# A gated mix of two attention blocks: the gate's sums and the output weights' operands made in the prologue by ScalarE and GpSimd

## The chip, the cores and the metric

The kernel runs on one core of a Trainium2 chip. The metric is device time in microseconds for one launch. The kernel before took 2869.4 us (median of three runs, 2869.4 to 2871.16). The profiled execution is one more run of the same program.

## The reference

One input x of 2048 tokens and width 1024 goes through two blocks of 32 heads (32 wide each), and a gate per token mixes them. All data is f32.

```python
x = A_x
g = _sigmoid((x * gate_w).sum(-1, keepdims=True))
a = _A_ref(x, A_wqkv, A_wo)    # linear attention: phi(q) (phi(k)^T v) / (phi(q) . sum phi(k)), then @ wo
b = _B_ref(x, B_wqkv, B_wo)    # softmax attention: softmax(q k^T / sqrt(32)) v, then @ wo
return g * a + (1 - g) * b
```

phi(t) is t + 1 for t > 0 and exp(t) otherwise, plus 1e-6.

## The kernel before, in words

**Products.** Every large product is made of three matmuls (`three`, L150): each operand is split into a rounded high part, by a ScalarE copy to float32r, and a low part, by a subtraction (`split`, L294 to L296). Block B's q and k and the output product of block B use a form of Strassen's scheme with seven products (`PRODUCTS`; for the output `OPS`, L356), so their operands are sums and differences of quarter blocks.

**Prologue.** Two halves of the tokens, J = 0 and 1. For each, a *v pass* of eight steps k (`v_pass`, L401) puts the first half of B's v into all eight banks, while VectorE splits the pieces of x and makes their sums (`sides`, `split_sides`). Then come eight *quads* (`quad`, L449): each makes q or k for two groups of four heads out of seven products of 12 matmuls, in six banks in turn. While quad f runs, `beside` steps through generators, one step after each product: the weights of quad f + 1 (`quad_weights`), the last sums of x, the spills of the x pieces to HBM (`spill_rest`), and `wo_sums` (L499). That last one loads blocks of the output weights `b_wo` over GpSimd's DMA queue into the two halves of `zrep`, makes the four sums S1 to S4 with GpSimd, and stores them raw to HBM (`so_d`); a one-column copy by ScalarE and one by GpSimd (L506, L507) pace it. Weights of v and of the quads lie in a ring of half tiles (`RINGW`, 14 places). At the end of each v pass ScalarE copies the eight banks of v out (`v_out`, L359) into P1, C11, H11 and W2, four tiles that also hold the quads' sums.

**Main loop.** A planner at trace time (L1831 on) keeps a modelled time per engine (`T`) and puts together four streams in one order for every engine: `linear` (the rest of v, then block A's "kv", "q" and "o" chunks), `maxima` (scores of a head, whose row maxima VectorE reduces out of a bank, L1193), `heads_` (scores again, exp by ScalarE at L1333 into big tiles, the product with v at L1480; GpSimd adds up the exponentials at L1411 and L1415) and `output`. VectorE's work that isn't urgent is put in by `defer` with a cost. Beside these, three helpers are asked in every turn. `gate_step` (L530), in the kv chunks: it loads half rows of x and lets VectorE multiply and sum them with `gate_w` (L553), 32 times, at least 12 us apart, and ends with the sigmoid (L540 to L544). `pre_split` (L1511), in the o chunks: it loads one of 28 blocks of the seven operands of the output product, lets ScalarE copy the high part (L1530) and VectorE subtract (L1533, planned at 0.9 us like L553), and stores both to `wo_d`; all DMAs of `dma` (L168) stand on SP's one queue. `load_w_op` (L1565) loads the finished operands, two tiles of 1 MB each, into big tiles as these become free.

**Output.** For each of eight pairs of token tiles, X11 and T1 need the even blocks of o (`load_e`, into `raw_e` = mid0 and mid1), the other five products also the odd ones (`load_l`). The first NE = 3 pairs of X11 and T1 are made before the last head is done (L1723). `load_e(1)` is issued in the last unit of `linear` (L1042), and `load_e(2)` after `load_l(0)` in `output` (L1722).

Of the kernel before, what the change touches and what calls it, by code (L numbers as in the profile page):

```python
# [19 lines left out]
P = 128  # L20
DH = 32
# [18 lines left out]
GATE_STEP = 12.0  # L40
NE = 3
AHEAD_X = 3
PIECE_STEP = 13.0
# [6 lines left out]
def kernel(  # L50
# [3 lines left out]
    x: bass.AP,  # L54
# [70 lines left out]
    big = [None if i in (15, 19, 20) else big_tile(i, F32R) for i in range(NBIG)]  # L125
# [218 lines left out]
    RAW_BIG = (19, 20, 15)  # L344
    assert all(RINGW[NK + 2 * i + half] == (b, half) for i, b in enumerate(RAW_BIG) for half in range(2))
# [9 lines left out]
    so_d = {m: [dram.tile([P, C], F32, name=f"so{m}_{i}") for i in range(KH)] for m in ("S1", "S2", "S3", "S4")}  # L355
# [7 lines left out]
    def vcols(c):  # L363
        return [(2 * D + c * C, C)]

# [126 lines left out]
    def wo_piece(m, i):  # L492

        if m[0] == "S":
            return so_d[m][i]
        half, l = int(m[1]) - 1, int(m[2]) - 1
        return b_wo[(2 * i + l) * P:(2 * i + l + 1) * P, half * C:(half + 1) * C]

    def wo_sums():  # L499

        z0, z1 = halves(zrep)
        tokens = count()

        def step(*fns):
            n = next(tokens) % (C // DH)
            nc.scalar.copy(dn[0][:, n:n + 1], eps)  # L506
            nc.gpsimd.tensor_copy(dn[1][:, n:n + 1], dn[0][:, n:n + 1])  # L507
            for fn in fns:
                fn()
            for _ in range(4):  # L510
                yield

        load = lambda z, m, i: lambda: nc.gpsimd.dma_start(z, wo_piece(m, i))
        store = lambda m, z, i: lambda: nc.gpsimd.dma_start(so_d[m][i], z)
        add = lambda *a: lambda: nc.gpsimd.tensor_add(*a)
        sub = lambda *a: lambda: nc.gpsimd.tensor_sub(*a)
        for i in range(KH):
            yield from step(load(z0, "W21", i), load(z1, "W22", i))
            yield from step(add(z1, z0, z1), load(z0, "W11", i), store("S1", z1, i))
            yield from step(sub(z1, z1, z0), load(z0, "W12", i), store("S2", z1, i))  # L520
            yield from step(sub(z0, z0, z1), load(z1, "W21", i), store("S4", z0, i))
            yield from step(load(z0, "W11", i))
            yield from step(sub(z0, z0, z1), store("S3", z0, i))

    sums_w = wo_sums()

    gate_w_t = [mid[8], mid[9]]
    gate_at, gate_n = [0.0], [0]

    def gate_step():  # L530

        n = gate_n[0]
        if lin_kind[0] != "kv" or gate_at[0] is None or gate_at[0] > T["pe"] or n > 2 * NT:
            return
        if n == 0:
            for i, w in enumerate(gate_w_t):
                dma(w, bass.AP(tensor=gate_w.tensor, offset=gate_w.offset + i * C, ap=[[0, P], [1, C]]))
        gate_n[0] += 1
        if n == 2 * NT:
            nc.vector.tensor_add(g_sb, g_sb, omg_sb)  # L540
            nc.scalar.activation(g_sb, g_sb, AF.Exp, scale=-1.0)
            nc.vector.tensor_scalar_add(g_sb, g_sb, 1.0)
            nc.vector.reciprocal(g_sb, g_sb)
            nc.vector.tensor_scalar(omg_sb, g_sb, -1.0, 1.0, op0=ALU.mult, op1=ALU.add)  # L544
            use("dve", 0.4)
            return
        t, i = divmod(n, 2)
# [35 lines left out]
    for k in range(4):  # L583
        load_block(k)
# [1323 lines left out]
```

## Time and profile before

| what | value |
|---|---|
| median of the runs | 2869.4 us |
| the profiled execution, its own time | 2867.15 us |
| its span, first to last instruction | 2865.4 us |
| DMA | 471.57 MB, mean 165 GB/s |
| L553 (gate sums, VectorE) | 32 of 1970 ns on average |
| L1533 (low parts of output operands, VectorE) | 28 of 1586 ns |
| L516 and L515 (sums of output weights, GpSimd) | 12 of 1476 ns and 4 of 1284 ns |

Line numbers (L553) are those of the kernel before. "Busy" is the time an engine spends in instructions; matmuls overlap, so TensorE's time per matmul is read from counts in a window rather than from the mean of one. A window row gives the window's length, then for each engine its busy time and the number of instructions, the granted share of TensorE's clock, the busy share of the DMA engines and GB/s. A wait row reads "who waited <- for whom: total, times, longest". In a timeline row the first number is the start, the second the duration.

### The profile page before, as it was taken

Reading aid. Unit: us, or ns where it says so; the run is one execution under the profiler, and the core shown is the slowest. Engines: PE = TensorE matmul, PEld = TensorE weight load, DVE = VectorE, ACT = ScalarE, POOL = GpSimd, SP = SyncE. Lnnn points to the kernel's source line nnn. Section 1 sums busy time; section 2 is a strip of 40 time slices with the busy share of each in tenths; the row PEclk is TensorE's granted clock in tenths of the full one; section 3 lists DMA queues with packets and bytes.
Section 4 is the critical chain, followed back from the end, with each engine's and each line's share of the span. In section 5 each row is a group of like instructions: output and inputs, shape, how many; then the busy total and the mean of one; then the engine's idle time right before and its main releaser. Section 6 shows DMA issues by size and latency. Waiting matters only on the chain.

```text
span 2865.4 us, 46944 instructions
## 1 busy us (share of the span) xinstructions
PE 2814.4 (98%) x15848; PEld 2043.1 (71%) x15848; DVE 2397.1 (84%) x3838; ACT 1629.8 (57%) x3084; POOL 2007.3 (70%) x1010
## 2 busy tenths in 40 slices
PE   9999999999999999999999999999999999999999
PEld 8888888667766776666667767767766666666587
DVE  7877747889999999898988888878888998887588
ACT  5334321666666666666756666666666666556422
POOL 0211240799999999999889988889889889787000
PEclk9999999999999999999999999999999999999999
DMA  8977776444433344343434344455675667555764
GB/s 288 285 251 247 251 222 191 138 104 110 135 102 106 104 122 121 97 120 105 136 89 107 99 126 150 147 178 177 185 218 172 196 192 215 150 159 173 246 213 155
DMA packets 412379, 471.57 MB, mean 165 GB/s; under 512 B 107486, under 2 KB 235742, under 8 KB 410348
## 3 DMA queue, kind: packets, MB, share of 16 engines
q1 hardware_dynamic: 394092, 441.84, 49.9%
q0 software_dynamic: 18048, 26.75, 4.9%
q8 instruction: 126, 2.06, 0.3%
q14 instruction: 113, 0.93, 0.1%
HBM read 322.17 MB, written 131.86 MB: 158 GB/s over the span
## 4 chain that ended last, share of the span: by engine, by line
PE 89%; DVE 7%; DMA 2%; issue 1%; SPq 0%; ACT 0%; ACTq 0%; DVEq 0%
PE bank L1330 15%; PE bank L1188 15%; PE bank L154 14%; PE bank L157 14%; PE bank L159 14%; PE bank L1480 14%; DVE mx L1193 3%; DVE mid L553 1%; DVE mid L1533 1%; DVE bank L1262 1%; DVE bank L1431 1%; PE bank L1252 0%; PE bank L978 0%; SPq L171 0%; PE bank L867 0%
## 5 line engine op out<-in xcount | busy, mean ns | idle before, releaser
L1415 POOL TENSOR_TENSOR big<-big,big 128x512 f32<-128x512 f32 (+2 forms) x694 | 1659.3, 2395 | 118.1 <-ACT big L1333 75.7
L1193 DVE TENSOR_REDUCE mx<-bank 128x1 f32<-128x512 f32 x2048 | 1308.9, 683 | 260.4 <-PE bank L1188 257.8
L1333 ACT ACTIVATE big<-bank 128x512 f32<-128x512 f32 x2048 | 1180.1, 603 | 468.2 <-PE bank L1330 408.3
L1330 PE MATMUL bank<-big,big 128*128 128x512 f32 x1888 | 746.4, 397 | 17.5 <-DMA big<-ml 6.4
L1188 PE MATMUL bank<-big,big 128*128 128x512 f32 x1888 | 744.5, 394 | 18.1 <-DVE mx L1193 16.8
L154 PE MATMUL bank<-big,big 128*128 128x512 f32 x1576 | 617.9, 392 | 9.4 <-ACT big L295 7.7
L157 PE MATMUL bank<-big,big 128*128 128x512 f32 x1576 | 615.8, 391 | 0.0
L159 PE MATMUL bank<-big,big 128*128 128x512 f32 x1572 | 614.5, 391 | 0.1
L1330 PEld LDWEIGHTS bank<-big,big 128*128 128x128 f32 x1888 | 355.5, 189 | 149.8 <-issue 42.5
L1480 PE MATMUL bank<-big,mid 128*32 128x512 f32 x4096 | 456.0, 595 | 0.0
L1188 PEld LDWEIGHTS bank<-big,big 128*128 128x128 f32 x1888 | 356.3, 189 | 98.3 <-DVE mx L1193 22.5
L154 PEld LDWEIGHTS bank<-big,big 128*128 128x128 f32 x1576 | 297.3, 189 | 75.6 <-ACT big L295 8.6
L159 PEld LDWEIGHTS bank<-big,big 128*128 128x128 f32 x1572 | 296.0, 188 | 63.7 <-DMA big<-xs 0.9
L157 PEld LDWEIGHTS bank<-big,big 128*128 128x128 f32 x1576 | 297.2, 189 | 61.4 <-DVE big L296 0.2
L1480 PEld LDWEIGHTS bank<-big,mid 128*32 128x32 f32 x4096 | 143.1, 110 | 267.4 <-issue 267.1
L1431 DVE TENSOR_TENSOR bank<-bank,big 128x512 f32<-128x512 f32 x364 | 251.6, 691 | 5.0 <-ACT big L1333 2.9
L507 POOL COPY dn<-dn 128x1 f32<-128x1 f32 x24 | 16.1, 671 | 304.3 <-ACT dn L506 304.3
L295 ACT CAST big<-mid 128x512 fp32r<-128x512 f32 (+1 forms) x157 | 92.7, 617 | 124.5 <-DVE mid L1631 66.9
L1411 POOL TENSOR_TENSOR big<-big,big 128x1536 f32<-128x1536 f32 (+1 forms) x31 | 123.9, 3997 | 46.9 <-ACT big L1333 46.8
L296 DVE TENSOR_TENSOR big<-mid,big 128x512 fp32r<-128x512 f32 (+1 forms) x157 | 106.2, 691 | 57.9 <-ACT big L295 57.6
L154 PE MATMUL bank<-big,xh 128*128 128x512 f32 x376 | 148.0, 394 | 0.8 <-DMA xh<-xs 0.8
L157 PE MATMUL bank<-big,xh 128*128 128x512 f32 x376 | 147.6, 393 | 0.0
(150 smaller groups left out, 2226.3 us busy)
## 6 DMA issues: line engine op xcount, KB each, us to landing
big<-xs SPq DMA_DIRECT2D x288, 256.0 KB
big<-qk SPq DMA_DIRECT2D x690, 64.0 KB
xh<-xs SPq DMA_DIRECT2D x144, 256.0 KB
qk<-mid SPq DMA_DIRECT2D x128, 256.0 KB
big<-oA SPq DMA_DIRECT2D x84, 256.0 KB
xs<-big SPq DMA_DIRECT2D x64, 256.0 KB
oA<-mid SPq DMA_DIRECT2D x64, 256.0 KB
big<-big POOLq DMA_DIRECT2D x50, 256.0 KB, 5.4
```

Of the source, the lines that this page charges most:

```text
L154: yield nc.tensor.matmul(ps, sh, mh_, start=(kt == 0), stop=False)
L157: yield nc.tensor.matmul(ps, sh, ml_, start=False, stop=(late and last))
L159: yield nc.tensor.matmul(ps, sl, mh_, start=False, stop=last)
L296: eng.tensor_sub(lo, src, f32(hi))
L1188: nc.tensor.matmul(bank[b], q[:, t % TPC * P:(t % TPC + 1) * P], k[:, j * C:(j + 1) * C], start=True, stop=True)
L1193: nc.vector.tensor_reduce(m[:, t, j:j + 1], bank[b], AX.X, ALU.max)
L1330: nc.tensor.matmul(bank[b], k[:, t * P:(t + 1) * P], q_cols(h, j), start=True, stop=True)
L1333: nc.scalar.activation(pr_t[i][:, j * C:(j + 1) * C], bank[b], AF.Exp, scale=SCALE)
L1411: nc.gpsimd.tensor_add(lacc[:, :qp], pr(0)[:, :qp], pr(1)[:, :qp])
L1415: nc.gpsimd.tensor_add(lacc[:, sl], lacc[:, sl], pr(t)[:, sl])
L1431: nc.vector.tensor_add(lacc[:, qp:] if t == NT - 1 else l_b[:, :n], l_b[:, :n], src)
L1480: nc.tensor.matmul(av_b[j * DH:(j + 1) * DH, :], v[:, t, :], pr(t)[:, j * C:(j + 1) * C], start=(t == 0), stop=(t == NT - 1))
```

## The change

The gate. `gate_step` and the input x in token order go. The host hands over `gate_w` as 128 x 8, and it is loaded once. In both v passes ScalarE multiplies each raw piece of x^T (features on the partitions) by its column of `gate_w`, and GpSimd adds these up in the halves of `zrep` (`gate_add`): 16 copies and 14 additions in each half J. In quad 0, after its third product, eight matmuls of f32 with one column of ones sum over the partitions into bank 6 (`gate`). So that the products may be read before `sides` overwrites the pieces, `sides` and `split_sides` of the first v pass come one step later.

The output weights. `wo_sums` and `pre_split` become `wo_parts`: in the quads of each half J, for two of the four i, ScalarE copies each of the seven operands' high part, GpSimd subtracts, and GpSimd's queue stores both to `wo_d`. There is one pair of places for high and low, the second half of big15, which leaves the ring with 13 places. One piece is made every three steps (`PIECE_STEP`). The spills of x take seven steps for every four parts.

The output. `load_e(1)` goes to a second pair of tiles and is issued beside `load_e(0)`, `load_e(2)` where `load_e(1)` was, ahead of `load_l(0)`. S2 and S4 are loaded when `load_l(0)` has been issued, and S4, S2 stand ahead of S3 in the list.

```diff
-GATE_STEP = 12.0
-PIECE_STEP = 13.0
+PIECE_STEP = 3
...
-    RINGW = [(14, 0), (14, 1), (16, 0), (16, 1), (17, 0), (17, 1), (18, 0), (18, 1), (19, 0), (19, 1),
-             (20, 0), (20, 1), (15, 0), (15, 1)]
+    RINGW = [(16, 0), (16, 1), (17, 0), (17, 1), (19, 0), (19, 1), (14, 0), (14, 1), (20, 0), (20, 1), (15, 0),
+             (18, 0), (18, 1)]
...
+    gate_wt, gate_sum, gate_b = kvb[:, 0, :NK], halves(zrep), bank[6]
+    def gate(J):
+        yield
+        yield
+        for t in range(2 * TPC):
+            nc.tensor.matmul(gate_b[:, t:t + 1], gate_sum[t // TPC][:, t % TPC * P:(t % TPC + 1) * P], ones[:, :1],
+                             start=True, stop=True)
+        g = g_sb[:, 2 * TPC * J:2 * TPC * (J + 1)]
+        nc.scalar.activation(g, gate_b[:, :2 * TPC], AF.Exp, scale=-1.0)
+        yield
...
+    gate_t = [C11, H11, P1, W2]
+    def gate_add(raws, k):
+        for jj in range(2):
+            acc, raw, w = gate_sum[jj], raws[jj + 2 * (k % 2)], gate_wt[:, k:k + 1]
+            to = gate_t[(2 * k + jj) % len(gate_t)] if k else acc
+            nc.scalar.activation(to, raw, AF.Copy, scale=w)
+            if k:
+                nc.gpsimd.tensor_add(acc, acc, to)
...
-    def wo_sums():
+    def wo_parts(i0, i1):
         z0, z1 = halves(zrep)
+        hi_w, lo_w = (big[15][:, i * C:(i + 1) * C] for i in (2, 3))
+        def load(z, m, i, **add):
+            if i < i1:
+                nc.gpsimd.dma_start(z, wo_piece(m, i), **add)
+        def part(m, i, z):
+            nc.scalar.copy(hi_w, z)
+            nc.gpsimd.tensor_sub(lo_w, z, f32(hi_w))
+        def out(m, i):
+            for p, src in enumerate((hi_w, lo_w)):
+                nc.gpsimd.dma_start(wo_d[m][p][:, i * C:(i + 1) * C], f32(src))
+            for _ in range(PIECE_STEP):
                 yield
...
+        for i in range(i0, i1):
+            part("W11", i, z1)
+            nc.gpsimd.tensor_sub(z1, z1, z0)
+            load(z0, "W22", i, accum_op=ALU.add)
+            yield from out("W11", i)
+            part("S3", i, z1)
+            load(z1, "W11", i)
+            yield from out("S3", i)
+            part("S1", i, z0)
+            nc.gpsimd.tensor_sub(z0, z0, z1)
+            load(z1, "W12", i)
+            yield from out("S1", i)
+            part("S2", i, z0)
+            yield from out("S2", i)
+            part("W12", i, z1)
+            nc.gpsimd.tensor_sub(z1, z1, z0)
+            load(z0, "W22", i)
+            yield from out("W12", i)
+            part("S4", i, z1)
+            load(z1, "W11", i + 1)
+            yield from out("S4", i)
+            part("W22", i, z0)
+            load(z0, "W21", i + 1)
+            yield from out("W22", i)
...
     def spill_rest(J):
+        part = 0
         for name in ("X11", "X21", "X22"):
-            yield from spill(J, name)
+            for _ in spill(J, name):
+                part += 1
+                for _ in range(2 if part % 4 else 1):
+                    yield
...
+        gate_add(raw_x0[k // 2], k)
         v_pass(0, k, V_BANKS[0], range(TPC) if k == 0 else None)
-        if k % 2:
-            sides(raw_x0[k // 2], k // 2)
-        elif k:
-            split_sides(raw_x0[k // 2 - 1], 0, k // 2 - 1)
+        if k >= 2:
+            i = k // 2 - 1
+            if k % 2:
+                split_sides(raw_x0[i], 0, i)
+            else:
+                sides(raw_x0[i], i)
...
-    quads(0, lambda: load_pair(raw_x1[0], 1, 0), spill_rest(0), sums_w)
+    quads(0, lambda: load_pair(raw_x1[0], 1, 0), spill_rest(0), gate(0), wo_parts(0, KH // 2))
...
                 if k == 0 and n + 3 == len(units):
                     load_e(0)
+                    load_e(1)
...
-                    load_e(1)
+                    load_e(2)
...
-              "S2": lambda: over["lin"], "S4": lambda: over["lin"],
+              "S2": lambda: raw_l[0], "S4": lambda: raw_l[0],
...
-    w_next = ["W11", "S1", "W12", "S3", "S4", "S2", "W22"]
+    w_next = ["W11", "S1", "W12", "S4", "S2", "S3", "W22"]
```

More of the change, by code (lines that the diff above doesn't have):

```diff
@@ L342, in halves @@
         return [t[:, i * C:(i + 1) * C] for i in range(t.shape[1] // C)]
-    RAW_BIG = (19, 20, 15)
-    assert all(RINGW[NK + 2 * i + half] == (b, half) for i, b in enumerate(RAW_BIG) for half in range(2))
+    RAW_BIG = (20, 15, 18)
+    assert not {b for b, _ in RINGW[:NK]} & set(RAW_BIG)
     raw_big = [halves(big_tile(b, F32)) for b in RAW_BIG]
@@ new lines, in wo_parts @@
+        yield
+        yield
+        yield
+        load(z1, "W11", i0)
+        load(z0, "W21", i0)
+        for _ in range(PIECE_STEP):
+            yield
+        for i in range(i0, i1):
[22 more added lines that the diff above has]
+            yield from out("W22", i)
@@ L726, in split_v1 @@
         split(wpart(k, 0), wpart(k, 1), raw, nc.vector)
-    quads(1, lambda: load_v1(raw_a, range(KH)), spill_rest(1), sums_w)
-    for _ in sums_w:
-        pass
+    quads(1, lambda: load_v1(raw_a, range(KH)), spill_rest(1), gate(1), wo_parts(KH // 2, KH))
     load_v1(raw_b, range(KH, NK))
```

115 lines of the change are left out of this document (23 added, 92 removed).

## The prediction, on record before the change was run

> **What bounds the kernel now.** I read the page first, for who ends last.
>
> ```profile
> span 2865.4 us, 46944 instructions
> PE 2814.4 (98%) x15848; PEld 2043.1 (71%) x15848; DVE 2397.1 (84%) x3838; ACT 1629.8 (57%) x3084; POOL 2007.3 (70%) x1010
> PE 89%; DVE 7%; DMA 2%; issue 1%; SPq 0%; ACT 0%; ACTq 0%; DVEq 0%
> ```
>
> TensorE sets the end: it is idle for 51 us (2865.4 less 2814.4), and the chain leaves it for VectorE for 7% of the span. So the change can win no more than those idle stretches, and what the clock loses after them. The view of cores gives the second, and a table of windows says where both lie.
>
> ```profile
> core 0: 2865.4 us, clock 0.994
> ```
>
> ```profile
> core 0: us, PE busy (x) PEld busy (x) DVE busy (x) ACT busy (x) POOL busy (x), PEclk, DMA share, GB/s
> 0.00:50.00 50.00, 48.93 (x211) 40.94 (x212) 40.15 (x66) 27.43 (x49) 0.71 (x6) 1.00 0.91 300
> 50.00:200.00 150.00, 150.00 (x664) 124.20 (x663) 112.33 (x168) 57.69 (x114) 30.97 (x43) 1.00 0.82 262
> 200.00:246.00 46.00, 46.00 (x204) 38.10 (x203) 35.77 (x57) 21.71 (x38) 0.00 (x0) 1.00 0.77 248
> 246.00:400.00 154.00, 154.00 (x681) 127.52 (x680) 116.27 (x176) 58.82 (x115) 44.06 (x56) 1.00 0.75 242
> ...
> 500.00:1500.00 1000.00, 978.96 (x6210) 683.74 (x6211) 898.45 (x1487) 647.50 (x1255) 907.57 (x447) 0.99 0.41 114
> 1500.00:2080.00 580.00, 579.77 (x3396) 415.21 (x3395) 494.27 (x819) 380.47 (x730) 525.58 (x229) 1.00 0.49 146
> 2080.00:2600.00 520.00, 503.34 (x2801) 343.06 (x2800) 452.80 (x693) 326.46 (x584) 446.97 (x196) 0.99 0.64 187
> ...
> 2700.00:2760.00 60.00, 52.29 (x217) 42.05 (x216) 37.96 (x59) 14.56 (x26) 0.00 (x0) 0.94 0.84 274
> ```
>
> Clock 0.994 over the span is 17 us lost. The prologue (to 400 us) has no idle TensorE at all; one matmul costs 154/681 = 0.226 us there, so a step of the v pass (24) 5.4 us and a product of a quad (12) 2.7 us. Idle time stands in three places: 21.0 us in 500 to 1500, where the gate's sums run; 16.7 us in 2080 to 2600, where the pieces of the output weights are split; 7.7 us at 2700 to 2760, the start of the output. Between them, 1500 to 2080, with neither, it is 0.2 us in 580. That clean stretch is the strongest argument for a gain. Next, what ended TensorE's waits, and which VectorE instructions are long:
>
> ```profile
> PE bank L1188 <- DVE mx L1193: 16.8, 7, 3.1
> PE bank L154 <- ACT big L295: 7.7, 2, 6.5
> PE bank L1330 <- DMA big<-ml: 6.4, 2, 5.2
> PE bank L1330 <- DVE mx L1193: 4.4, 4, 2.5
> PE bank L1330 <- DVE mid L1265: 3.9, 4, 1.4
> ```
>
> ```profile
> L553 DVE SCALAR_TENSOR_TENSOR mid<-mid,mid x32: 681/1589/4790, 519.0 to 1442.5; 128x512 f32<-128x512 f32 x32
> ```
>
> ```profile
> L1533 DVE TENSOR_TENSOR mid<-mid,mid 128x512 fp32r<-128x512 f32 x28 | 44.4, 1586 | 0.0
> L542 DVE TENSOR_SCALAR g_sb<-g_sb 128x16 f32<-128x16 f32 x1 | 3.3, 3260 | 0.3 <-ACT g_sb L541 0.3
> ```
>
> ```profile
> 1171.19 4.67 DVE L553 SCALAR_TENSOR_TENSOR mid<-mid,mid 128x512 f32<-128x512 f32 x1
> ```
>
> ```profile
> 1171.04 4.26 POOL L1411 TENSOR_TENSOR big<-big,big 128x1536 f32<-128x1536 f32 x1
> ```
>
> The two last fences are VectorE and GpSimd at the same moment: the gate's sum, 0.68 us at best, sits until GpSimd's long add has ended (1171.04 + 4.26 = 1175.3). The row maximum queued behind it (L1193) then frees its bank late. The hand-written order gave each of these 0.9 us.
>
> **The change, part by part.**
>
> *Gate out of the kv stage.*
>
> ```profile
> 500.00:519.00 19.00, 16.53 (x69) 12.64 (x69) 12.12 (x21) 11.49 (x23) 4.32 (x3) 1.00 0.87 284
> ```
>
> 32 L553 and L542 go, with 32 loads of x. Idle 21.0 us less the 2.5 us (19.00 - 16.53) that lie before the first L553 at 519: 18.5. Clock: 0.99 over 1000 us can be 5 to 15 us; I take 6. **Gain 24** (18 to 28). The Trainium skill ("TensorE: Matmul & The Clock Gate", HAM oscillation) lets the clock fall only after idle gaps over about 3.4 us; by it these waits, 3.1 us at most, would cost no clock and the term would be 18. The row's 0.99 speaks against it.
>
> *Pieces out of the o stage.*
>
> ```profile
> 2424.85 1.26 SPq L171 DMA_DIRECT2D woS<-mid  x2
> ...
> 2428.65 1.46 SPq L171 DMA_DIRECT2D big<-mh  x2
> ```
>
> 28 copies, 28 L1533, 28 loads and 56 stores on SP's queue go. Of 16.7 us idle, 6.4 wait for the DMAs of ml, which follow those of mh at 2428.65 on SP; before them stand the pieces' stores with 1.26 us among others, and I count 2 us of the wait as theirs. The other 10.3 are waits for VectorE, 9 of them put down to L1533. With 4 us of clock (0.99 over 520): **gain 15** (9 to 20).
>
> *Blocks of o earlier.* At 2714 ScalarE waits for a block that SP issued late:
>
> ```profile
> 2698.66 8.71 SPq L171 DMA_DIRECT2D xh<-oB  x3
> 2707.42 3.75 SPq L171 DMA_DIRECT2D mid<-oB  x4
> ```
>
> ```profile
> 2714.57 0.62 ACT L295 CAST big<-mid 128x512 fp32r<-128x512 f32 x1 [12.68 <-DMA mid<-oB]
> ```
>
> load_e(2) is the last of those; it stood behind load_l(0), whose xh places were not yet free. Now it goes ahead of both load_l(0) and S2, S4. The stretch lost 7.7 us idle and 0.06 x 60 = 3.6 of clock. What is late next: the 8 MB of S4, S2, S3 and W22 (two tiles of 128x2048 f32 each), which must now land 11 us sooner at 274 GB/s (84% DMA). **Gain 8** (3 to 11).
>
> *Gate matmuls.* 16 of f32 with one moving column, each two records as L961's are.
>
> ```profile
> L1480 PE MATMUL bank<-big,mid 128*32 128x512 f32 x4096 | 456.0, 595 | 0.0
> L978 PE MATMUL bank<-ident,mid 128*128 128x128 f32 x128 | 19.4, 274 | 0.0
> L961 PE MATMUL bank<-mid,ones 128*128 128x256 f32 x8 | 2.4, 378 | 0.0
> ```
>
> Per record 0.11, 0.15 and 0.30 us; 32 records make 3.6 to 9.6; L978 is nearest in its weights. They run in the prologue, where TensorE has no gap. **Loss 5.**
>
> *Gate sums in the two v passes.* Per pass 16 ScalarE copies and 14 GpSimd adds of 128x512, the size of these:
>
> ```profile
> L515 POOL TENSOR_TENSOR zrep<-zrep 128x512 f32<-128x512 f32 x4 | 5.1, 1284 | 0.0
> ```
>
> ```profile
> 152.71 0.68 DVE L434 TENSOR_TENSOR xh<-mid,xh 128x512 f32<-128x512 f32 x1
> 153.31 0.69 DVE L296 TENSOR_TENSOR big<-extra,big 128x512 fp32r<-128x512 f32 x1
> 153.91 1.78 DVE L437 TENSOR_TENSOR mid<-xh,mid 128x512 f32<-128x512 f32 x1
> ```
>
> ```profile
> 153.40 1.75 POOL L516 TENSOR_TENSOR zrep<-zrep 128x512 f32<-128x512 f32 x1
> ```
>
> An add of GpSimd amid VectorE's subtractions costs VectorE 1.1 us (1.78 against 0.69). In the first pass VectorE has no room:
>
> ```profile
> 10.00:47.50 37.50, 37.50 (x167) 31.03 (x167) 36.84 (x59) 21.64 (x40) 0.00 (x0) 1.00 0.96 319
> ```
>
> ```profile
> 46.55 2.03 ACT L360 COPY mid<-bank 128x512 f32<-128x512 f32 x4
> ...
> 240.77 2.63 ACT L360 COPY mid<-bank 128x512 f32<-128x512 f32 x4 [0.75 <-PE bank L159]
> ```
>
> ScalarE frees the banks of v (L360) only after the last casts of quad 0's weights, which follow VectorE; and the copies write P1, C11, H11, W2, where the gate's products now lie until GpSimd has added them. So at least 13 adds must be done: 13 x 1.1 = 14.3 us late. The first copy ended at 47.1, and TensorE, with 208 of its 211 records done, wanted the bank at 50 - 3 x 0.226 = 49.3: slack 2.2, **loss 12** (0 if GpSimd fits between, 14 at most). In the second pass the records 1073 and on (of 211 + 664 + 204 at 246 us) want bank 2 at 244.5, the third copy, ended by 242.7: slack 1.8. VectorE works 35.77 of 46 us there, so part of the adds fits; but the adds and the wait for the stores of P1 and W2 (some 2 us) delay the loads of quad 0's weights too. **Loss 10** (0 to 15). Both waits are long enough to drop the clock as at 2700 (3.6 us there); **loss 4** for both. The Trainium skill ("SBUF — State Buffer", Who interferes with whom) says that a VectorE instruction with two SBUF inputs and a GpSimd one that reads SBUF hold the shared port whole, one after the other; it speaks against this change: at a whole 1.28 us per add both passes together would lose 5 us more. The 1.78 us row bears out most of it.
>
> *Pieces in the quads.* Per block i seven pieces, each a ScalarE copy (0.62), a GpSimd subtraction (1.3, 1.75 when contended), two stores, one pair of places. The next copy must wait for the landing of the last store of hi. The old stores and loads beside zrep took:
>
> ```profile
> DMA to landing us min/median/max: 2.3/4.8/6.4
> ```
>
> Copy to landing: three pieces with a second subtraction and a load 4.4 + L, three with a load 2.8 + L, one 2.2 + L, so 23.8 + 7L per block, against 21 products of TensorE, 56.7 us. L 4.8 gives 57.4: just even. With 40 more stores of 256 KB (10 MB over 300 us, 35 GB/s on 242 to 262) L may be 5 to 5.5: 2 to 6 us late per block, four blocks, and each half hides about 6 us, since a product's bank is wanted again three products after it is released. The 24 extra subtractions fall on VectorE, busy 75% there, and are hidden. **Loss 3** (0 to 20).
>
> **Sum:** 24 + 15 + 8 = 47 won, 5 + 12 + 10 + 4 + 3 = 34 lost: 13 us less. The profiled execution took 2867.15 us (span 2865.4), so 2854 for one like it; the median shown is 2.25 us above it, so **2856 us**.
>
> **Rivals.** *Slower, by the pair hi and lo.* If stores land in 6.4 us, the maximum above, a block takes 68.6 us, 11.9 more than TensorE's; four blocks less 12 us hidden lose 36 instead of 3: 2889. It decides from L = 5.7 on, where the pieces lose 16 and the 13 us are eaten. For it: DMA share is 0.82 where the pieces go, and the stores triple. Against it: the median of 4.8, and spills now spread over more of the quads. *All hidden.* If GpSimd's adds slip between VectorE's instructions and the pass absorbs them, only the gate's 5 us remain lost: 2869.4 - 47 + 5 = 2827. For it: TensorE has no gap in 400 us, so the order has some reserve. Against it: 36.84 of 37.5 us. *Cancelled.* If other VectorE work takes the place of L553 and L1533 in front of the maxima, half of 39 us stays: 2876; with the losses a little smaller, no change, 2869. Against it: the clean 580 us, in which VectorE is 85% busy too. *It doesn't do as it says* in one point: S3 and W22 still load late, so that the output wins 3 instead of 8; 2861, inside the forecast.
>
> **Chances.** The forecast with its bounds (2840 to 2862) 0.42; all hidden 0.2; cancelled 0.17 (0.15 of it within 0.2%); slower by the pair or by both passes at their upper ends 0.21. Faster means below 2863.7: 0.62; within 0.2% (5.7 us, about what a measurement of this kernel tells from no change) 0.15; slower 0.23. The range takes in the hidden case and most of the slow one: 2828 to 2885.
>
> **What would show it.** Windows of the changed kernel: TensorE idle in 500 to 1500 below 5 us, in 2080 to 2600 below 8; no wait over 2 us on ACT L295 in the output. Against that, a wait of TensorE for ScalarE's copies out of v near 50 and near 245, about 10 us each, and a prologue some 34 us longer. If the prologue ends within 8 us of before, the port term is wrong; if the kv stage still idles 15 us, it was not L553; if ScalarE waits on the stores of hi for over 3 us each, the pair decides.

## The result, and the profile after

The changed kernel takes **2875.45 us** (median of 12 runs, 2868.85 to 2881.64), the kernel before 2869.4 in the same session (12 runs, 2865.07 to 2872.05): ratio 1.0021, 95% interval 1.0011 to 1.003. It is slower by 6 us where 13 us less were forecast. The profiled execution took 2881.64 us, the slowest of its twelve, so what follows adds up to +14.5 us and not to +6.

The page of the changed kernel, the same three lines that the prediction began with:

```profile
span 2879.9 us, 46927 instructions
PE 2815.7 (98%) x15880; PEld 2051.5 (71%) x15880; DVE 2348.8 (82%) x3745; ACT 1649.3 (57%) x3093; POOL 2073.2 (72%) x1078
PE 80%; DMA 3%; DVE 1%; issue 1%; SPq 1%; ACT 0%; POOL 0%; ACTq 0%; DVEq 0%; POOLq 0%
```

TensorE still sets the end, and still has 64 us without work. They have moved, as the table of windows shows (busy time and instructions of PE, PEld, DVE, ACT, POOL, then granted clock, DMA share, GB/s):

```profile
0.00:50.00 50.00, 46.12 (x188) 36.44 (x189) 41.10 (x46) 30.94 (x54) 23.55 (x20) 0.97 0.71 234
...
420.00:500.00 80.00, 76.63 (x323) 62.07 (x322) 37.76 (x54) 21.17 (x38) 37.62 (x55) 0.96 0.82 242
500.00:1500.00 1000.00, 996.87 (x6273) 709.81 (x6272) 859.42 (x1442) 628.35 (x1217) 860.15 (x430) 1.00 0.41 113
...
2080.00:2600.00 520.00, 516.70 (x2966) 355.26 (x2959) 434.71 (x696) 326.84 (x579) 454.90 (x202) 1.00 0.55 152
2700.00:2760.00 60.00, 52.03 (x239) 38.74 (x238) 31.96 (x50) 17.63 (x33) 0.00 (x0) 0.91 0.83 280
```

In the two stages that the change was to clear, TensorE is now almost full at clock 1.00: from 500 to 1500 it idles 3.1 us in place of 21.0, from 2080 to 2600 3.3 in place of 16.7. The start of the output is as bad as it was. What is new stands in the prologue. TensorE's waits in the changed kernel (us in total, times, longest) and the four matmuls that waited longest:

```profile
PE bank L152 <- ACT mid L357: 17.4, 2, 8.9
PE bank L152 <- ACT big L293: 12.8, 2, 8.0
PE bank L152 <- DVE mid L506: 11.1, 2, 6.0
PE bank L152 <- DMA xh<-xs: 5.4, 2, 3.1
```

```profile
63.28 0.80 PE L152 MATMUL bank<-big,big 128*128 128x512 f32 x1 [8.49 <-ACT mid L357]
...
171.16 0.76 PE L152 MATMUL bank<-big,big 128*128 128x512 f32 x1 [6.01 <-DVE mid L506]
...
291.86 0.79 PE L152 MATMUL bank<-big,big 128*128 128x512 f32 x1 [8.90 <-ACT mid L357]
...
2736.03 0.79 PE L152 MATMUL bank<-big,big 128*128 128x512 f32 x1 [7.97 <-ACT big L293]
```

L357 is the copy that frees a bank of v at the end of each v pass (L360 before), L506 is the sum by which VectorE empties the bank of a quad's third product, a bank that quad 5 of a half waits for, and L293 is the cast of a split. No wait for the row maxima is left.

A ledger finds the same matmul, by its count (without the gate's own), in both traces and compares its start time. A stage has the same matmuls in both, some in another order:

| stretch | lost (+) or won (-), us | forecast |
|---|---|---|
| first v pass | +13.8 (its end at 49.5, now 63.3) | +12 |
| quad 0 of both halves: gate matmuls, and slow matmuls behind the passes | +6.6 | +5, and 4 of clock |
| quads 1 to 7, both halves | +11.0 and +8.9 | +3 |
| second v pass | +18.5 | +10 |
| first linear chunk (v), after the quads | +6.5 | 0 |
| kv stage | -28.6 | -24 |
| q stage | +2.6 | 0 |
| o stage | -25.4 | -15 |
| output | +0.6 | -8 |
| sum | +14.5 | -13 |

In quad 0 the gate's matmuls themselves take 1.84 us in each half, 3.7 in all (the first half's here); the other 2.9 us are matmuls behind the long wait at the end of a pass, at a granted clock of 0.50 until 66.1 and until 294.8:

```profile
72.93 1.84 PE L370 MATMUL bank<-ones,zrep 128*128 128x1 f32 x16
```

The two stages won more than the idle time in their windows. Cut at the same matmuls, the kernel before (first fence) and the changed one (second) show why; the rows are the kv and the o stage:

```profile
504.00:1705.40 1201.40, 1181.25 (x7487) 827.70 (x7486) 1076.71 (x1790) 785.81 (x1522) 1100.75 (x546) 1.00 0.41 113
...
2121.70:2695.60 573.90, 557.94 (x3146) 374.11 (x3145) 488.77 (x747) 358.12 (x647) 450.40 (x190) 0.99 0.61 183
```

```profile
569.30:1742.10 1172.80, 1170.86 (x7487) 827.10 (x7486) 1016.76 (x1722) 784.46 (x1521) 1089.58 (x546) 1.00 0.40 108
...
2161.00:2709.50 548.50, 547.33 (x3146) 371.53 (x3145) 451.12 (x719) 347.43 (x619) 441.70 (x190) 1.00 0.53 152
```

The same 3146 matmuls of the o stage have 14.8 us less of idle time (16.0 to 1.2), and are themselves 10.6 us shorter (557.94 to 547.33). In the kv stage it is 18.2 and 10.4. Part of this is the clock: a wait can be followed by slow matmuls (the section on why the prediction failed shows one). The rest isn't told apart here.

### The profile page after: what moved, and what is told of

It is laid out like the page before. It is cut to its first block, busy times and chain, and to the rows that moved or that the text cites. A ratio compares the mean times of both kernels' runs of the same rounds, so it can differ in the third digit from the quotient of the medians.

```text
span 2879.9 us, 46927 instructions
## 1 busy us (share of the span) xinstructions
PE 2815.7 (98%) x15880; PEld 2051.5 (71%) x15880; DVE 2348.8 (82%) x3745; ACT 1649.3 (57%) x3093; POOL 2073.2 (72%) x1078
## 4 chain that ended last, share of the span: by engine, by line
PE 80%; DMA 3%; DVE 1%; issue 1%; SPq 1%; ACT 0%; POOL 0%; ACTq 0%; DVEq 0%; POOLq 0%
PE bank L1358 16%; PE bank L1216 16%; PE bank L1508 15%; PE bank L152 10%; PE bank L155 10%; PE bank L157 10%; DMA woS<-big 1%; DMA v<-mid 1%; PE bank L1280 1%; SPq L169 1%; PE bank L1006 0%; PE bank L895 0%; DMA xh<-mid 0%; DMA xh<-xs 0%; DVE big L294 0%
## 5 line engine op out<-in xcount | busy, mean ns | idle before, releaser
L1443 POOL TENSOR_TENSOR big<-big,big 128x512 f32<-128x512 f32 (+2 forms) x694 | 1641.7, 2370 | 108.2 <-ACT big L1361 65.3
L152 PEld LDWEIGHTS bank<-big,big 128*128 128x128 f32 x1576 | 299.1, 190 | 112.5 <-ACT mid L357 18.2
L294 DVE TENSOR_TENSOR big<-mid,big 128x512 fp32r<-128x512 f32 (+1 forms) x157 | 119.5, 777 | 61.2 <-ACT big L293 61.1
L533 POOL TENSOR_TENSOR big<-zrep,big 128x512 fp32r<-128x512 f32 x28 | 37.2, 1330 | 171.6 <-ACT big L532 94.1
L293 ACT CAST big<-mid 128x512 fp32r<-128x512 f32 (+1 forms) x157 | 92.5, 616 | 108.0 <-DVE mid L1627 66.7
```

Of the source, the lines that this page charges most:

```text
L152: yield nc.tensor.matmul(ps, sh, mh_, start=(kt == 0), stop=False)
L294: eng.tensor_sub(lo, src, f32(hi))
L1443: nc.gpsimd.tensor_add(lacc[:, sl], lacc[:, sl], pr(t)[:, sl])
```

## Experiments

The first theory, from that ledger: **(a)** GpSimd's additions for the gate hold VectorE up and make both v passes late; **(b)** ScalarE, waiting for the stores of the one pair hi and lo to land, makes quad 5 late; **(c)** the output's start is bound by something that loading blocks of o earlier doesn't touch. The rivals: any added work in the passes does it, GpSimd's subtractions in the quads do it, or the new order of loads does it. Ratios are to the kernel before in the same session; "us" is the median.

### What makes the v passes late

**e1**, no additions:

```diff
             nc.scalar.activation(to, raw, AF.Copy, scale=w)
-            if k:
-                nc.gpsimd.tensor_add(acc, acc, to)
```

> The changed kernel without the 28 GpSimd additions of the gate's sums (the gate's sums are then those of the first block alone); ScalarE's 32 copies, their places P1 and W2, and the gate's matmuls stay. Theory: the additions, amid VectorE's dense subtractions of the two v passes, hold VectorE up (1.7 to 1.8 us instead of 0.69 each), and that is 11 of the 13.8 us lost in the first pass and about 10 of the 18.5 in the second: 2854 us (2849 to 2860), TensorE's 8.65 us stall at 63 gone. Rival: ScalarE's copies and their wait for the stores of P1 and W2 carry the loss of the passes: within 5 us of the changed kernel, 2870 to 2876, and the stall at 63 stays.

Measured: 2844.47 us, ratio 0.9928 (0.9909 to 0.9946). The first pass ends at 48.8, 0.7 us *earlier* than in the kernel before, with all of ScalarE's 16 new copies in it; the second pass loses 5.8 in place of 18.5. The theory's sign holds, and its size was short: by the ratios (1.0021 to 0.9928) e1 wins 27 us on the changed kernel, not 21. The same group of VectorE's subtractions in the first pass, in the changed kernel and in e1 (busy us, mean ns, then idle time):

```profile
L294 DVE TENSOR_TENSOR big<-big,big 128x512 fp32r<-128x512 f32 x22 | 21.8, 1040 | 3.7 <-ACT big L293 3.7
```

```profile
L294 DVE TENSOR_TENSOR big<-big,big 128x512 fp32r<-128x512 f32 x22 | 13.9, 687 | 3.6 <-ACT big L293 3.6
```

The count and the shapes are the same; the mean is 1040 ns with the additions and 687 without.

**e9**, additions without copies:

```diff
-            to = gate_t[(2 * k + jj) % len(gate_t)] if k else acc
-            nc.scalar.activation(to, raw, AF.Copy, scale=w)
             if k:
-                nc.gpsimd.tensor_add(acc, acc, to)
+                nc.gpsimd.tensor_add(acc, acc, raw)
```

> The changed kernel with GpSimd's 28 additions of the gate reading the raw blocks of x directly, and without the 28 copies of ScalarE that weight them (the gate's sums then lack their weights). No addition waits for a copy and no copy for a place. Theory: it is the additions beside VectorE's subtractions that cost the time: the first pass again loses 12 to 14 us (TensorE's stall at 63 stays), and the second wins back the 8 us of the wait for P1 and W2: 2867 us (2863 to 2872). Rival: it is the chain copy, addition, free place, next copy on ScalarE's queue that is late: as without any additions, 2844 to 2852 us.

Measured: 2866.76 us, ratio 0.9995 (0.9985 to 1.0004), on the theory's number. Without the 28 copies the first pass loses 13.4, as much as with them; the second loses 11.4. So the chain of copies and places is not the cause in the first pass. The windows of the first pass in the changed kernel, in e9 and in e1, each from 10 us to its end:

```profile
10.00:63.00 53.00, 42.09 (x173) 32.76 (x171) 50.78 (x59) 30.27 (x54) 22.84 (x14) 0.93 0.68 227
```

```profile
10.00:62.90 52.90, 42.74 (x172) 33.66 (x170) 51.02 (x59) 22.63 (x41) 23.17 (x14) 0.93 0.69 231
```

```profile
10.00:48.80 38.80, 38.80 (x173) 32.02 (x172) 36.90 (x59) 29.79 (x55) 0.00 (x0) 1.00 0.93 311
```

Read the third and the fifth pair of figures: the same 59 VectorE instructions take 36.90 us beside no GpSimd work and 50.78 or 51.02 beside 14 additions, 1.0 us more for each addition. The Trainium skill ("SBUF — State Buffer", Who interferes with whom) calls the port that the two engines share an exclusive lock; these rows agree in kind, at 1.0 us for an addition whose shortest took 1.3 us (L390).

In the second pass 18.5 less 11.4 is what the copies add: they write P1 and W2, whose last products are still being stored. The changed kernel's ScalarE and VectorE there:

```profile
242.76 0.72 ACT L388 ACTIVATE mid<-xh,kvb 128x512 f32<-128x512 f32 x1 [7.21 <-DMA qk<-mid]
```

```profile
244.82 0.69 DVE L405 TENSOR_TENSOR xh<-xh,mid 128x512 f32<-128x512 f32 x1 [8.36 <-ACT mid L388]
```

ScalarE's copy waits 7.2 us for a store, and VectorE 8.4 us for the copy. The prediction gave this wait "some 2 us". ScalarE's waits for these stores are shorter where the pieces are out of the quads (2.1 us in e6, below, against 7.8 in all here), and there the pass loses 12.7. So the pieces, too, lengthen the second pass; how they delay those stores isn't shown.

**e3**, the sums by VectorE alone:

```diff
-            to = gate_t[(2 * k + jj) % len(gate_t)] if k else acc
-            nc.scalar.activation(to, raw, AF.Copy, scale=w)
             if k:
-                nc.gpsimd.tensor_add(acc, acc, to)
+                nc.vector.scalar_tensor_tensor(acc, raw, w, acc, op0=ALU.mult, op1=ALU.add)
+            else:
+                nc.scalar.activation(acc, raw, AF.Copy, scale=w)
```

> The changed kernel with each of the 28 later gate pieces done by one VectorE multiply-add (scalar_tensor_tensor) into the sum in place of ScalarE's copy and GpSimd's addition; everything else as changed. Theory of the additions' hold on VectorE: an instruction of VectorE's own takes 0.7 us where an addition of GpSimd costs 1.1, and the wait for the places P1 and W2 goes, so the passes get back 4 and 12 us: 2860 us (2855 to 2867). Rival: what counts in the passes is any work on VectorE's side at 98% busy, so that 0.7 us more per piece costs as much as before: 2870 to 2876 with the gain of the places at most 5.

Measured: 2858.26 us, ratio 0.9965 (0.9954 to 0.9977): as the theory had it, and already faster than the kernel before. The passes lose 7.6 and 8.8. In e9, which hasn't the copies either, they lose 13.4 and 11.4. So 28 more instructions of 0.75 us on VectorE, full as it is, cost less than 28 additions on GpSimd beside it.

### What each half of the change is worth

**e4**, the gate back in the kv stage (the core of the diff):

```diff
     def gate_add(raws, k):
 
+        return
         for jj in range(2):
...
+        gate_step()
         fold_now()
```

> The changed kernel with the gate as it was before: 32 VectorE sums over loads of x in the kv stage; no gate piece and no gate matmul in the prologue. Theory: the gate's part of the change costs the prologue 38 to 40 us (13.8 + 18.5 in the passes, 6.5 in the matmuls) and wins 28.6 in the kv stage, so that undoing it wins about 10: 2865 us (2859 to 2870), the kv stage again with some 21 us of idle TensorE between 500 and 1500. Rival: the kv stage's gain is the change's whole gain and the passes are late for the new order of loads and sides, not for the gate: slower than the changed kernel, 2880 to 2900.

Measured: 2871.02 us, ratio 1.0014 (1.0005 to 1.0024), 1 us above the expected interval. By the ledger the prologue and the first linear chunk lose 26.2 without the gate and 65.3 with it, and the kv stage wins nothing without it: 39.1 paid for 28.9 in these profiles. By the ratios e4 wins only 2 us on the changed kernel, and the two intervals overlap.

**e6**, the pieces back in the o stage:

```diff
-    def wo_parts(i0, i1):
+    def wo_sums(i0, i1):
...
+        pre_split()
         load_w_op()
```

> The changed kernel with the pieces of the output weights as they were before (GpSimd sums S1 to S4 beside the quads, hi and lo made in the o stage by ScalarE and VectorE, with their loads and stores on SyncE's queue); the gate stays in the prologue as changed. Theory: the pieces cost the prologue about 23 us (quads 5 and 7 of the first half 10, quad 5 of the second 8, the first products after it 6) and won 25 in the o stage: undoing them gives 2874 to 2881 us, the stalls of TensorE at 171 and 399 gone, and some 16 us of idle in the o stage back. Rival (the prediction's step): pieces in the quads cost 3: 2890 to 2897.

Measured: 2870.15 us, ratio 1.0006 (0.9996 to 1.0015). Neither number: the pieces cost 30.0 by the ledger (65.3 less 35.3), more than the 23 expected, and won 24 in the o stage, where e6 loses all but 1.2 of the 25.4. The rival (3 us) is out by far. So **each half of the change gives back about what it wins**: the pieces alone (e4) leave the kernel 4 us slower than before, and the gate alone (e6) can't be told from no change.

### What makes quad 5 late

The chain behind TensorE's wait of 6.01 us at 171.16 in the changed kernel, on ScalarE and then on VectorE:

```profile
166.15 0.62 ACT L532 CAST big<-zrep 128x512 fp32r<-128x512 f32 x1 [3.88 <-DMA woW<-big]
...
167.31 1.64 DVE L294 TENSOR_TENSOR big<-mid,big 128x512 fp32r<-128x512 f32 x1 [2.36 <-ACT big L293]
...
170.32 0.69 DVE L506 TENSOR_TENSOR mid<-bank,mid 128x512 f32<-128x512 f32 x1
```

ScalarE's copy of a piece waits for a store to land, the next cast stands behind it, VectorE waits for that cast, and the sum that frees the bank comes late.

**e2**, stores that don't hold the pair:

```diff
-            for p, src in enumerate((hi_w, lo_w)):
-                nc.gpsimd.dma_start(wo_d[m][p][:, i * C:(i + 1) * C], f32(src))
+            for p in range(2):
+                nc.gpsimd.dma_start(wo_d[m][p][:, i * C:(i + 1) * C], wo_piece("W11", i))
```

> The changed kernel with its 56 stores of pieces reading a block of b_wo in DRAM in place of the pair hi and lo (as many stores of as many bytes; the output's operands are then wrong), so that ScalarE's next copy does not wait for the landing of the last. Theory: the wait of ScalarE for the landing of the stores (55 us over 28 pieces) makes ScalarE and then VectorE late in quads 5 of both halves and costs about 18 us: 2858 us (2853 to 2864), the stalls of TensorE at 171 and 399 gone. Rival: the 52 GpSimd subtractions that the pieces do hold VectorE up, and the wait is hidden: no change, 2870 to 2876.

Measured: 2850.29 us, ratio 0.9939 (0.9924 to 0.9954). Quads 1 to 7 lose 0.0 us in both halves in place of 11.0 and 8.9, with all of GpSimd's subtractions still there. The rival falls. The ledger also has the second v pass at 13.8 in place of 18.5 and the first linear chunk at 0.1 in place of 6.5, neither of which the expectation counted.

**e8**, a second pair, at the price of one place of the ring:

```diff
-    RINGW = [(16, 0), (16, 1), (17, 0), (17, 1), (19, 0), (19, 1), (14, 0), (14, 1), (20, 0), (20, 1), (15, 0),
-             (18, 0), (18, 1)]
+    RINGW = [(16, 0), (16, 1), (17, 0), (17, 1), (19, 0), (19, 1), (14, 0), (14, 1), (20, 0), (20, 1), (18, 0),
+             (18, 1)]
...
+            hi_w, lo_w = pairs[0]
+            pairs.reverse()
```

> The changed kernel with two pairs of places for hi and lo, taken in turn (the second pair is a place of the weights' ring, which then has 12 in place of 13). Theory: ScalarE's wait for the landing of the stores of hi (3.6 to 8.0 us a store) is what the pieces cost: with a second pair a piece's copy waits for the stores of the piece before the last, 9 us earlier, the stalls of quads 5 go, and the time is 2855 us (2850 to 2861). Rival one: GpSimd's 52 subtractions hold VectorE up: 2872 to 2877. Rival two: the ring with 12 places makes the weights of a quad late and eats the gain: over 2864, with new waits of TensorE for VectorE in the quads.

Measured: 2917.68 us, ratio 1.0168 (1.0153 to 1.0183): rival two, far beyond what it named. TensorE's waits in e8:

```profile
PE bank L152 <- ACT big L293: 43.2, 17, 8.8
...
PE bank L157 <- DVE big L294: 11.7, 11, 2.5
```

Of the seventeen waits for casts fifteen stand at the second product of a quad, one in nearly every quad. With 12 places the weights of the next quad come late, as the rival had it. On the pair itself this run says nothing.

**e10**, the same places and the same work, the stores issued earlier:

```diff
             nc.scalar.copy(hi_w, z)
+            nc.gpsimd.dma_start(wo_d[m][0][:, i * C:(i + 1) * C], f32(hi_w))
             nc.gpsimd.tensor_sub(lo_w, z, f32(hi_w))
+            nc.gpsimd.dma_start(wo_d[m][1][:, i * C:(i + 1) * C], f32(lo_w))
...
-            for p, src in enumerate((hi_w, lo_w)):
-                nc.gpsimd.dma_start(wo_d[m][p][:, i * C:(i + 1) * C], f32(src))
```

> The changed kernel with the stores of a piece issued earlier on GpSimd's queue: that of hi right behind ScalarE's copy, that of lo right behind its subtraction, both ahead of the piece's second subtraction and load. Same work, same places, same ring of 13. Theory of the landing wait: ScalarE gets the place of hi back 2 to 4 us earlier per piece, which is most of its 55 us of waits; the stalls of quads 5 shrink or go: 2859 us (2851 to 2866). Rival: the subtractions of GpSimd hold VectorE up and the wait is hidden: 2872 to 2877.

Measured: 2853.69 us, ratio 0.9961 (0.9946 to 0.9976). The answer for ScalarE's copy of a piece, L532, in the changed kernel (its waits, us and times) and in e10:

```profile
L532 ACT CAST big<-zrep x28: 612/621/623, 90.3 to 439.3; 128x512 fp32r<-128x512 f32 x28
...
its engine sat idle before it (us, times) until:
  DMA woS<-big: 30.6, 12
  DMA woW<-big: 24.7, 10
```

```profile
L532 ACT CAST big<-zrep x28: 613/616/622, 90.0 to 415.7; 128x512 fp32r<-128x512 f32 x28
...
its engine sat idle before it (us, times) until:
  DMA woS<-big: 0.6, 1
```

55.3 us of waits in 22 copies became 0.6, and quads 1 to 7 lose 0.0 us in both halves. Theory (b) is shown from both sides: e2 takes the wait away, e10 shortens what stands before it.

### Where the output's 8 us went

**e5**, the kernel before with the output part alone:

```diff
                     load_e(0)
+                    load_e(1)
...
-    raw_e = (mid[0], mid[1])
+    raw_e = [(mid[0], mid[1]), (mid[3], mid[4])]
...
-    w_next = ["W11", "S1", "W12", "S3", "S4", "S2", "W22"]
+    w_next = ["W11", "S1", "W12", "S4", "S2", "S3", "W22"]
```

> The kernel before with only the change's output part: the second and third blocks of o load earlier (into mid 3 and 4 and before load_l(0)), S2 and S4 may load earlier and the output weights load in the order W11, S1, W12, S4, S2, S3, W22. Theory: the start of the output is bound by the landing of the bytes of the weights and blocks (DMA share 0.84 before, 0.83 after the change in 2700 to 2760), so the order alone moves nothing: 2867 to 2872 us, with 6 to 9 us of idle TensorE there again. Rival (the prediction's step): the block that ScalarE waited 12.7 us for comes in time and the stretch wins 8: 2859 to 2863.

Measured: 2869.99 us, ratio 1.0003 (0.9994 to 1.0012): nothing, as theory (c) had it. The block that ScalarE waited 12.7 us for is in time, and the next one isn't. SyncE's queue and ScalarE in e5:

```profile
2704.37 2.54 SPq L171 DMA_DIRECT2D big<-woS  x4
...
2708.65 6.58 SPq L171 DMA_DIRECT2D xh<-mid  x1
```

```profile
2720.82 0.62 ACT L295 CAST big<-xh 128x512 fp32r<-128x512 f32 x1 [6.44 <-DMA xh<-mid]
```

The issue of the last head's rows of the block (xh<-mid, a transfer of 16 KB from tile to tile, `load_rest`) takes 6.6 us on the queue, behind 4 MB of weights. Two runs on top of the version with both cures (n1, below) tell whether it is the queue or the bytes. **e11** and **e12**:

```diff
-            dma(to[LAST, KH - 1], avs[j * DH:(j + 1) * DH, i * P:(i + 1) * P])
+            nc.gpsimd.dma_start(to[LAST, KH - 1], avs[j * DH:(j + 1) * DH, i * P:(i + 1) * P])
```

> The version with both cures (2838 us, 0.9906 of the kernel before) with one edit: the small transfers of the last head's rows into the blocks of o (load_rest) are issued on GpSimd's queue, which is idle there, in place of SyncE's, where one of them waits 5.2 us behind the weights S2 and S3 before it is issued. Queue theory: ScalarE's wait of 6.9 us for it shrinks by most of those 5 us: 2833 us (2830 to 2835), ratio to before 0.988 to 0.9895. Rival, the DMA engines are full (share 1.04 at 2680 to 2690): the rows land no earlier, within 2 us of 2838, ratio 0.990 to 0.9915.

```diff
-              "S2": lambda: raw_l[0], "S4": lambda: raw_l[0],
-              "S3": lambda: st_done[0] == steps,
+              "S2": lambda: raw_l[0] and not rest_left, "S4": lambda: raw_l[0],
+              "S3": lambda: st_done[0] == steps and raw_l[0] and not rest_left,
-              "W22": lambda: over["head"] and pr_idle(slot(H - 1, NT - 6), slot(H - 1, NT - 5))}
+              "W22": lambda: over["head"] and raw_l[0] and not rest_left and pr_idle(slot(H - 1, NT - 6), slot(H - 1, NT - 5))}
```

> The same version with another edit: the weights S2, S3 and W22 (2 MB each) load only when the last head's rows have been sent for, on the same queue. Theory of the bytes ahead: the rows land some 5 us earlier and ScalarE's wait shrinks, but the weights are late in their turn; on balance 2834 us (2831 to 2837). Rival: the first product with S2 or S3 waits as long as the wait that goes: 2837 to 2845.

Measured: e11 **2831.58 us**, ratio 0.9879 (0.9862 to 0.9895), against 0.9906 for n1, the queue theory's number; e12 2840.15, 0.9906 (0.9891 to 0.9921), no gain. In e11 GpSimd issues the same transfer at once, and ScalarE's cast doesn't wait at all:

```profile
2678.06 0.55 POOL L1611 DMA_DIRECT2D xh<-mid  x1 [64.82 <-ACT mid L1671]
```

```profile
2685.72 0.62 ACT L293 CAST big<-xh 128x512 fp32r<-128x512 f32 x1
```

with the DMA engines as full as ever:

```profile
2680.00:2690.00 10.00, 8.81 (x38) 6.63 (x38) 4.47 (x8) 2.96 (x6) 0.10 (x1) 1.00 1.04 382
```

By the ledger the output is 8.6 us shorter in e11 than in the kernel before, and as long as there in e12; all four runs of e11 lie below all four of e12 in the same session. So theory (c), as e5's expectation put it (bound by bytes), is wrong: it was a small transfer's place in a queue. In e12 the rows are in time too, but the rows of block A's output (`ra`) now stand behind the weights. SyncE's queue, VectorE and ScalarE there:

```profile
2677.09 2.39 SPq L169 DMA_DIRECT2D big<-woS  x4
...
2681.66 0.85 SPq L169 DMA_DIRECT2D big<-ra  x2
```

```profile
2698.34 0.75 DVE L1680 SCALAR_TENSOR_TENSOR big<-mid,omg_sb,big 128x512 f32<-128x512 f32 x1 [9.00 <-DMA big<-ra]
```

```profile
2701.18 0.62 ACT L293 CAST big<-xh 128x512 fp32r<-128x512 f32 x1 [12.05 <-DVE xh L1627]
```

VectorE's wait for `ra` is 2.1 us in e11. On one queue the order here only chose who waited.

### Versions that follow

**n1** is e3 and e10 together.

> Both cures in one: the gate's sums by one VectorE multiply-add per piece, and the stores of hi and lo issued right behind the instructions that make them. Theory: the two losses lie in different stretches (passes and quads 5) and their cures add, 17 and some 16: 2842 us (2834 to 2850), faster than both kernels. Rival: VectorE's multiply-adds make the passes late by what the earlier stores win, so that no more than the larger of the two is seen: 2855 to 2860.

Measured: **2838.03 us**, ratio 0.9906 (0.9891 to 0.992): the cures add, since they lie in different stretches. Its first product of the first linear chunk starts at +23.6 against the kernel before (+58.8 in the changed kernel), and the kv and o stages keep their 28.7 and 25.7. With e11's edit, 1.2% below the kernel before, it is the fastest version here.

**n2** and **b2** put the gate's sums into the first linear chunk, n2 on e10's stores, b2 on the kernel before (the lines of b2; n2 has the same `gate_step`):

```diff
-        if lin_kind[0] != "kv" or gate_at[0] is None or gate_at[0] > T["pe"] or n > 2 * NT:
+        if lin_kind[0] not in ("v", "kv") or lin_done[0] < GATE_FROM or gate_at[0] > T["pe"] or gate_free[gate_n[0] % 2] is None or gate_free[gate_n[0] % 2] > T["pe"] or n > 2 * NT:
...
-        xn, to = mid[10], (g_sb, omg_sb)[i]
+        xn, to = gate_x[n % 2], (g_sb, omg_sb)[i]
```

In both, the two places of gate_x also hold v of the first two heads, which the loads of x overwrite, so that part of the attention is computed from other values; the amount of work is the same.

> The changed kernel with the stores of a piece issued earlier, and with the gate taken out of the prologue and put into the first linear chunk (v, between the quads and the kv stage), as VectorE sums over loads of x as in the kernel before, one each 2.6 us with two places in turn. Theory: VectorE is busy 50% there and GpSimd does no long additions, so the 32 sums cost nothing but the contention of their 8 MB of loads with those of x (DMA share 0.73 there): the gate's 33 us in the prologue go, the kv stage keeps its gain, 2830 us (2822 to 2842). Rival: the added loads make the x of the linear chunk late (a wait of 3.3 us for it is there already), 10 to 25 us: 2842 to 2860.

> The kernel before with one edit: the 32 sums of the gate run in the first linear chunk (v) in place of the kv stage, one each 2.6 us with two places in turn. Nothing else of the change. Theory: the kv stage's 18.5 us of idle TensorE and its clock go (the changed kernel won 28 there) and the chunk hides the sums: 2844 us (2838 to 2856). Rival: the loads of x collide with those of the chunk and half or more is given back: 2856 to 2868.

Measured: n2 2846.84 us, 0.9935 (0.9918 to 0.9951); b2 2858.99, 0.9973 (0.9963 to 0.9982). Both are faster than the kernel before, both by the rival's account. TensorE's first waits in n2:

```profile
PE bank L156 <- DMA xh<-xs: 10.0, 2, 8.8
...
PE bank L156 <- DMA big<-xs: 5.8, 2, 3.3
```

The chunk's own x comes late behind the gate's loads: n2 loses 19 us between its first product and the kv stage, b2 18. Compared with n1 (0.9906), the prologue, where x is in SBUF anyway, is the better place.

## Why the prediction failed, step by step

- **"Pieces in the quads, loss 3 (0 to 20)"** is the step that failed most: 20 us in the quads, and 30 for the pieces in all (e6), with what they add to the second v pass (5.8) and with some 6 in the first linear chunk, whose cause is open (below). Its formula came near and its L was too small. From a median of 4.8 for the old stores and loads it took 5 to 5.5, and said that from 5.7 on the pair decides. The stores of hi and lo in the changed kernel:

```profile
L537 POOL DMA_DIRECT2D woS<-big x32: 539/539/565, 104.6 to 433.5; - x32
...
DMA to landing us min/median/max: 2.8/5.7/8.0
```

  At L 5.7 its formula gives 16 us. The forecast stood on the near side of an edge that its own working had drawn. That each half would hide 6 us was an estimate with no row behind it.
- **"Gate sums in the two v passes", losses 12 and 10, clock 4**: 13.8 and 18.5, and 2.9 of clock in quad 0. In the first pass the mechanism is right and the size nearly so (VectorE held by the additions, ScalarE's copies of v late: e1 and e9). The second was mis-sized in two ways. "VectorE works 35.77 of 46 us there, so part of the adds fits" didn't happen: without them the pass loses 5.8 and not 18.5, so the 14 additions cost 12.7. And ScalarE's wait for a store was 7.2 us and not 2.
- **"Blocks of o earlier, gain 8 (3 to 11)"**: nothing. The step asked what would be late next, and looked at the bytes of the weights; the small transfer behind them on SyncE's queue is what was late (e5). With that one on another queue the 8 us are there (e11).
- **"Gate matmuls, loss 5"**: 3.7.
- **"Gate out of the kv stage, gain 24 (18 to 28)"**: right in mechanism, 28.6. Idle time is 18.2 of it (forecast 18.5), shorter matmul time 10.4 (forecast 6). **"Pieces out of the o stage, gain 15 (9 to 20)"**: 25.4, of which 14.8 are idle time (forecast 11) and 10.6 matmul time (forecast 4). It counted 2 of the 6.4 us of waits for ml as the pieces'; 1.2 of them are left. The 10.3 us that it calls waits for VectorE were 8.6 by the wait rows, the rest waits for other loads. Three rows of the kernel before, at the very wait that the prediction took as its example, and the window behind it:

```profile
1176.52 0.50 PE L1188 MATMUL bank<-big,big 128*128 128x512 f32 x1 [2.66 <-DVE mx L1193]
...
1178.51 0.63 PE L1188 MATMUL bank<-big,big 128*128 128x512 f32 x1
1178.93 0.63 PE L1330 MATMUL bank<-big,big 128*128 128x512 f32 x1
```

```profile
1178.00:1181.40 3.40, 3.40 (x9) 2.51 (x9) 3.40 (x7) 2.16 (x6) 1.52 (x2) 0.50 0.45 154
```

  From 1.5 us after a wait of 2.66 us on, the granted clock is 0.50 for 3.4 us, and the spacing 0.43 us in place of 0.23, for some eight matmuls. The Trainium skill ("TensorE: Matmul & The Clock Gate", HAM oscillation) gives about 3.4 us as the gap from which the clock falls; here 2.66 were enough.
- **The rivals.** What happened is "slower, by the pair hi and lo" in its mechanism, with 20 us in the quads where it has 36, together with a second v pass above its upper end; that the total is only 6 us up is because the two stages won 54 and not 39. "All hidden" and "cancelled" are out: the passes hide nothing, and the clean kv stage stayed clean.
- **The signs it named.** Idle time below 5 and 8 us in the two stages came (3.1, 3.3); the waits for ScalarE's copies of v came at 63 and 292 (8.5 and 8.9 us); "no wait over 2 us on ACT L295 in the output" didn't (8.0), nor a prologue only 34 us longer (58.8). One sign was set too high: the pair was to decide if ScalarE waits over 3 us each for the stores of hi. It waits 2.5 on average (55.3 in 22), and the pair decides all the same.

Open: the first linear chunk, where TensorE waits for loads of x. It loses 6.5 us in the profile of the changed kernel, 7.0 in e3, 5.9 in e10 and 3.7 in e9, and between -0.2 and 1.7 in e1, e2, e4, e5, e6, n1, e11 and e12. In e10 the waits for the pair are gone and the loss is there, so the pair alone doesn't explain it, and what does wasn't tried. The q stage's 2.6 us go with a wait of 2.28 us for a load of x (at 2120.77) and 3.4 us at clock 0.50 behind it; nothing was tried on them.

## What to carry to other kernels

Work moved to an engine that looks idle is priced on the engine that it slows: here one GpSimd addition cost VectorE's dense stream 1.0 us, more than the 0.75 us that the same work takes on VectorE itself. A place that is stored from is busy until the landing, so issue the store right behind the instruction that fills it, ahead of everything else on that queue: that alone was worth about 17 us here (ratios 1.0021 and 0.9961). And when a wait is to go, follow the queue past the transfer that was late to the next one, however small.

## What was not expected of the hardware

A wait of 2.66 us of TensorE was followed by 3.4 us at clock 0.50. The kernel before has seven such stretches' worth in the two stages that the change cleared, and the changed kernel none; at half the clock they are 12 of the 54 us won. The length of the wait alone doesn't decide: one of 1.67 us (at 2528.43) is followed by clock 0.50, one of 3.00 us (at 1465.99) is not. What decides was not looked into.

On SyncE's queue the issue of one transfer of 16 KB took 6.58 us behind large ones (5.15 in n1); on GpSimd's queue, with the DMA engines just as full, it took 0.55. That is the queue's doing and not the transfer's: in e11, where it has left SyncE's queue, the next two issues there (`ra`) take 6.88 us.
